# First batch's attention written as a function of its own, with k on two queues, w_in behind v, the second softmax in token halves, and weight conversions ordered behind h's copies

## The chip, the cores and the metric

The kernel runs on one core of a Trainium2 chip. The metric is the time of one execution in microseconds (us) on the device; the median of repeated runs is compared. Before the change the median of three runs is 793.76 us (792.74 to 795.01).

## The reference

Two computations follow each other. First, attention through 32 packed queries per head: with q, k, v of 8 batches, 8 heads, 576 tokens and 64 dimensions and p of 32 rows per head,

```python
def sm_attn(qq, kk, vv):
    s = scale * np.matmul(qq, kk.transpose(0, 1, 3, 2))
    s = s - np.max(s, axis=-1, keepdims=True)
    a = np.exp(s)
    a = a / (np.sum(a, axis=-1, keepdims=True) + 1e-09)
    return np.matmul(a, vv)
p_packed = sm_attn(p, k, v)
out = sm_attn(q, p_packed, p_packed)
```

Then a feed-forward layer on the 4608 tokens of 512 features, with w_in 512 x 2048 and w_out 2048 x 512, both handed over as float64:

```python
h = x @ w_in
sp = np.maximum(h, 0.0) + np.log1p(np.exp(-np.abs(h)))
g = h * erf(sp)
return (g @ w_out).astype(np.float32)
```

## The kernel before

**The algebra.** The second attention's output is a2 x pt, where pt is the packed result of one batch and a2 the second softmax. The kernel never makes x: it multiplies pt into w_in once per batch (w' = pt x w_in, four blocks of 512 columns, `w_prime`, L298) and then takes h = a2 x w' over 256 inner elements (`h_part`, L338). Matmul operands are split in a high and a low part (hi, lo; a2h, a2l; wph, wpl; gh, gl; woh, wol) and three products are summed.

**A unit of work** is one block of 128 of the 2048 inner features for one batch: 128 units. Each has 12 matmuls for h (two token halves of 288, six each), copies of h from PSUM by ScalarE (`hs`, L354), a gate (Softplus and Erf on ScalarE, the product and the split into gh and gl on VectorE, `gate_group`, L322), and 12 matmuls into four output accumulators (`o_part`, L368), some units later. Units are gated in groups; a group begins with two loads of ScalarE's function table. The last 64 of the 576 tokens of each unit go through memory (`rest`, written by SP in `split_g`, L313) and are multiplied for pairs of batches (`o_rest`, L387). The first two batches are worked in turns of 8 units (batch 0, 1, 0, 1), the others 16 units at a time.

**Attention of a batch** (`attention`, L149) is a generator of 14 stages: loads of p, k, v and q on SP's queue; scores `s` and their maximum, Exp and scaling (a1); transposes `t` and their copy to a1t; the product `p` with v and its copy to pt (L263); second scores `s` and their transposes to ta (L275); maximum and subtraction (L280, L281); Exp (L283); sum, reciprocal, product, transpose to tb, a2h (L293) and a2l (L294). Batch 0 runs it ahead of all else, with the first block of w_in loaded in two pairs of tiles (`load_w_in_pair`, L96): the first pair is sent between k and v, the second between v and q.

**Weights.** A float64 tile is loaded as 64-bit words and turned into float32 by `convert` (L88): one scaling on ScalarE (L91), which waits for the load, and three bit operations on VectorE (L92 to L94). A tile of w_out is also split (`split_w_out`, L116). The first four of these tiles go into free buffers of w' (`EARLY`), the others through two staging buffers (tag `wst`).

**What sets the order.** `PLAN` says after which unit each attention stage, w' block and weight load is written in the program, which units end a gate group (`ends`) and how many units later the outputs follow (`wait`). The Tile scheduler then orders each engine's queue by its own estimate of times; an engine executes its queue in that order. From unit 48 on (`strict`) TensorE's order is that of the program; ScalarE's table functions follow each other as written (`in_turn`).

Of the kernel before, what the change touches and what calls it, by code (L numbers as in the profile page):

```python
# [18 lines left out]
PLAN = {  # L19
    "att": {1: (1, 1, 2, 2, 3, 4, 4, 5, 5, 7, 7), 2: (15, 15, 19, 19, 20, 20, 22, 24, 25, 25, 25, 27, 28, 30)},  # L20
    "steady": (0, 0, 0, 1, 2, 2, 5, 6, 7, 9, 11, 11, 12, 13),
    "wp": (-1, 2, 6, 6, 14, 10, 22, 23),
    "wp_steady": (12, 14, 15, 20),
    "wi": {1: (0, 0, 2, 2), 2: (6, 9, 11, 11), 3: (11, 12, 14, 16)},
    "wo": (0, 1, 1, 2, 2, 3, 4, 6, 15, 15, 18, 20, 21, 22, 23, 26),
    "ends": (4, 5, 8, 12, 13, 16),
    "wait": (4, 1, 1, 1, 1),
    "strict": 48,
}
# [5 lines left out]
def tile_pack_attention_moe(ctx: ExitStack, tc: tile.TileContext, qT, kT, v, pT, w_in, w_out, out, rest):  # L35
# [51 lines left out]

    def convert(dst, low, high):  # L88

        bits = dst.bitcast(U32)  # L90
        nc.scalar.mul(dst, high.bitcast(F32), F64_SCALE)  # L91
        nc.vector.tensor_scalar(bits, bits, 3, None, op0=ALU.logical_shift_left)  # L92
# [1 line left out]
        nc.vector.scalar_tensor_tensor(bits, low, 29, bits, op0=ALU.logical_shift_right, op1=ALU.bitwise_or)  # L94
# [243 lines left out]
    def h_part(n, c):  # L338
# [8 lines left out]
        at_c = slice(c * HT, (c + 1) * HT)  # L347
        ps = ps_h.tile([P, 512], F32, name=f"h{b}_{f}_{c}", tag="ps_h")
        m = 0
        for r in range(2):  # L350
            for w, a in ((whi, ahi), (whi, alo), (wlo, ahi)):
                pe(nc.tensor.matmul(ps[:, 0:HT], w[:, r, fo:fo + P], a[:, r, at_c], start=(m == 0), stop=(m == 5)))  # L352
                m += 1
        nc.scalar.copy(hs[:, at_c], ps[:, 0:HT])  # L354
# [116 lines left out]
    gens[0], gens[1] = attention(0), attention(1)  # L471
    pairs = []
    next(gens[0])
    pairs.append(load_w_in_pair(0))
    next(gens[0])
    pairs.append(load_w_in_pair(2))
    next(gens[0])
    for _ in range(STAGES - 3):
        next(gens[0])
    for pair in pairs:  # L480
        if pair:
            convert(*pair)
    for _ in range(3):
        next(gens[1])
# [62 lines left out]
```

## Time and profile before

| | us |
|---|---|
| median of three runs (lowest, highest) | 793.76 (792.74, 795.01) |
| the profiled execution | 795.34 |
| its span, first to last instruction | 793.4 |
| TensorE busy in the span | 733.5 |
| ScalarE busy | 494.9 |
| VectorE busy | 435.5 |

The span is what the trace covers; the profiled execution's own time has 1.94 us more around it. PE is TensorE's matmul, PEld its weight load, DVE VectorE, ACT ScalarE, POOL GpSimd, SP the engine that issues most DMAs (SPq its queue). A timeline row reads: start, length, engine, line, operation, output <- inputs, shapes, count, and in brackets the idle time before it and what released it. The granted clock is TensorE's, as a share of full speed. In a row of a stretch each engine's busy time is followed by its count of instructions.

### The profile page before, as it was taken

The numbers are of one execution on the slowest core, as the hardware profiler recorded it, in microseconds if no ns is written. First come the engines' busy times: TensorE is split into PE (matmuls) and PEld (weight loads), VectorE is DVE, ScalarE is ACT, GpSimd is POOL, SyncE is SP. The second block draws the span as 40 slices with busy tenths as digits, with TensorE's granted clock in tenths as the row PEclk, the third lists the DMA queues.
The fourth block names the chain that finished last, engine by engine and source line by source line (L and its number), as shares of the span: only waits on it lengthen the run. The fifth ranks groups of instructions, "written<-read, shape, count | busy, mean of one in ns | idle before, by whom it ended". The sixth has DMA issues, their size and how long they took to land.

```text
span 793.4 us, 12893 instructions
## 1 busy us (share of the span) xinstructions
PE 733.5 (92%) x5008; PEld 577.0 (73%) x5008; DVE 435.5 (55%) x678; ACT 494.9 (62%) x802; POOL 8.0 (1%) x14
## 2 busy tenths in 40 slices
PE   3458978999999999999999999999999999999997
PEld 2237636777777877778877887778777788788885
DVE  3597987774575237653584236644484326744440
ACT  3169658787587636776676457676576556766731
POOL 0000000000100100000000000000000000000000
PEclk7568988999999999999999999999999999999999
DMA  9922463451532532025212332024212320003103
GB/s 310 313 104 83 150 189 92 121 189 45 151 58 64 113 99 69 16 60 170 67 41 66 117 96 69 16 59 147 90 41 64 117 66 12 16 14 98 41 21 119
DMA packets 66397, 74.77 MB, mean 94 GB/s; under 512 B 40224, under 2 KB 42272, under 8 KB 66336
## 3 DMA queue, kind: packets, MB, share of 16 engines
q1 hardware_dynamic: 65184, 71.86, 29.4%
q0 software_dynamic: 1152, 2.10, 1.8%
q8 instruction: 39, 0.64, 0.3%
q14 instruction: 22, 0.18, 0.1%
HBM read 54.00 MB, written 19.92 MB: 93 GB/s over the span
## 4 chain that ended last, share of the span: by engine, by line
PE 71%; ACT 11%; DMA 8%; DVE 6%; issue 2%; SPq 1%; DVEq 0%; ACTq 0%
PE o L374 37%; PE h L352 21%; PE or L398 5%; DMA v<-v 3%; DMA wi<-w_in 3%; PE wp L304 3%; ACT t L330 2%; PE p L258 2%; ACT L330 2%; ACT t L327 1%; ACT hs L354 1%; DMA g<-rest 1%; PE s L272 1%; ACT L327 1%; PE s L209 1%
## 5 line engine op out<-in xcount | busy, mean ns | idle before, releaser
L374 PE MATMUL o<-woh,gl 128*128 128x512 f32 x512 | 201.9, 394 | 1.1 <-DVE gl L317 1.0
L374 PE MATMUL o<-woh,gh 128*128 128x512 f32 x512 | 201.4, 403 | 1.6 <-ACT ob L379 1.1
L354 ACT COPY hs<-h 128x288 f32<-128x288 f32 x256 | 97.6, 398 | 168.5 <-PE h L352 167.3
L374 PE MATMUL o<-wol,gh 128*128 128x512 f32 x512 | 201.4, 393 | 0.0
L352 PE MATMUL h<-a2h,wph 128*128 128x288 f32 x512 | 155.4, 304 | 14.0 <-ACT hs L354 14.0
L332 DVE TENSOR_TENSOR hs<-t,hs 128x576 f32<-128x576 f32 x128 | 91.8, 754 | 114.1 <-ACT t L330 114.1
L352 PE MATMUL h<-a2l,wph 128*128 128x288 f32 x512 | 152.3, 298 | 1.6 <-DVE a2l L294 1.6
L352 PE MATMUL h<-a2h,wpl 128*128 128x288 f32 x512 | 152.0, 297 | 0.0
L352 PEld LDWEIGHTS h<-a2h,wph 128*128 128x128 f32 x512 | 96.8, 190 | 41.9 <-ACT hs L354 24.7
L374 PEld LDWEIGHTS o<-woh,gh 128*128 128x128 f32 x512 | 95.6, 188 | 43.1 <-issue 26.9
L374 PEld LDWEIGHTS o<-wol,gh 128*128 128x128 f32 x512 | 96.4, 188 | 25.0 <-issue 4.4
L316 DVE CAST gh<-hs 128x576 fp32r<-128x576 f32 x128 | 58.2, 456 | 100.1 <-PE o L374 95.4
L374 PEld LDWEIGHTS o<-woh,gl 128*128 128x128 f32 x512 | 96.5, 188 | 17.5 <-DVE gl L317 2.3
L352 PEld LDWEIGHTS h<-a2l,wph 128*128 128x128 f32 x512 | 97.1, 190 | 9.7 <-DVE a2l L294 2.0
L352 PEld LDWEIGHTS h<-a2h,wpl 128*128 128x128 f32 x512 | 97.3, 190 | 0.9 <-issue 0.9
L317 DVE TENSOR_TENSOR gl<-hs,gh 128x576 fp32r<-128x576 f32 x128 | 96.3, 754 | 2.3
L327 ACT ACTIVATE t<-hs 128x576 f32<-128x576 f32 x128 | 88.0, 687 | 2.8
L330 ACT ACTIVATE t<-t 128x576 f32<-128x576 f32 x128 | 78.1, 675 | 0.4
L304 PE MATMUL wp<-w_in_sb,pt 64*32 64x512 f32 x512 | 47.9, 642 | 4.8 <-DVE wpl L307 3.3
L307 DVE TENSOR_TENSOR wpl<-wp,wph 128x1024 fp32r<-128x1024 f32 x32 | 39.1, 1222 | 17.8 <-ACT wph L306 17.2
L327 ACT ACT_TABLE_LOAD x36 | 46.2, 1283 | 0.6
L330 ACT ACT_TABLE_LOAD x36 | 46.2, 1283 | 0.6
(84 smaller groups left out, 569.4 us busy)
## 6 DMA issues: line engine op xcount, KB each, us to landing
q<-qT SPq DMA_DIRECT2D x32, 288.0 KB, 4.3
v<-v SPq DMA_DIRECT2D x32, 256.0 KB, 4.1
wos<-w_out SPq DMA_DIRECT2D x16, 512.0 KB, 3.5
out<-ob SPq DMA_DIRECT2D x32, 256.0 KB, 2.2
g<-rest SPq DMA_DIRECT2D x16, 512.0 KB, 3.3
k<-kT SPq DMA_DIRECT2D x28, 288.0 KB, 3.9
wi<-w_in SPq DMA_DIRECT2D x12, 512.0 KB, 4.6
rest<-gh SPq DMA_DIRECT2D x128, 32.0 KB, 1.5
```

Of the source, the lines that this page charges most:

```text
L258: pe(nc.tensor.matmul(po[64 * r:64 * r + 64, NK * c:NK * c + NK], values[j][0:n, 64 * (2 * c + r):64 * (2 * c + r) + 64], a1t[0:n, j, r, N ...
L304: pe(nc.tensor.matmul(ps[NK * c:NK * c + NK, r, :], pt[b][64 * r:64 * r + 64, NK * c:NK * c + NK], w_in_sb[64 * r:64 * r + 64, c, j * FB:( ...
L307: nc.vector.tensor_tensor(lo[:], ps[:], hi[:], op=ALU.subtract)
L316: nc.vector.tensor_copy(ghi[:], hs[:])
L317: nc.vector.tensor_tensor(glo[:], hs[:], ghi[:], op=ALU.subtract)
L327: in_turn(nc.scalar.activation(t[:], hs[:], AF.Softplus))
L330: in_turn(nc.scalar.activation(t[:], t[:], AF.Erf))
L332: nc.vector.tensor_tensor(hs[:], t[:], hs[:], op=ALU.mult)
L352: pe(nc.tensor.matmul(ps[:, 0:HT], w[:, r, fo:fo + P], a[:, r, at_c], start=(m == 0), stop=(m == 5)))
L354: nc.scalar.copy(hs[:, at_c], ps[:, 0:HT])
L374: pe(nc.tensor.matmul(acc[b][x][:], gg[:, x * P:(x + 1) * P], w[:], start=(first and n == 0), stop=(last and n == 2)))
L398: pe(nc.tensor.matmul(acc["rest"], gg, w[:], start=(k == 0 and i == 0 and n == 0), stop=(k == NFB - 1 and i == PER - 1 and n == 2)))
```

## The change

Batch 0's attention becomes a function `first_attention` with its own statements in their own order; `attention` keeps the other batches. The second and fourth tile of k are sent by ScalarE's queue ahead of its table load. All of v is sent before both pairs of w_in. The first softmax keeps scores in PSUM as before, but sums and scales each half of the rows apart. The transposes are copied out by ScalarE and VectorE, one half each. The second softmax (maximum, subtraction, Exp, sum, product, transpose, a2h, a2l) runs once for each half of the tokens, and the first half of h needs the first half only; a2 has its halves outermost for that. The list `hold` takes the names of the last a1t copy, of the second a2h copy and of every copy of h; a conversion's start on ScalarE is ordered behind the last of them written so far, without a semaphore.

`PLAN` has new numbers. Batch 1's loads, scores and first softmax are written right behind batch 0's attention, its remaining stages after units 1 to 7 (before: scores from unit 1 on, end at unit 7). Units 0 and 1 are gated by themselves, and the first outputs follow after unit 6 instead of 7.

```diff
-    "wi": {1: (0, 0, 2, 2), 2: (6, 9, 11, 11), 3: (11, 12, 14, 16)},
-    "ends": (4, 5, 8, 12, 13, 16),
+    "wi": {1: (0, 0, 2, 3), 2: (7, 7, 10, 13), 3: (12, 14, 16, 16)},
+    "ends": (2, 5, 7, 9, 12, 14, 16),
+    "hold": 1,
...
     def convert(dst, low, high):
...
+        start = nc.scalar.mul(dst, high.bitcast(F32), F64_SCALE)
+        if hold:
+            follow(start, hold[-1])
...
+    def first_attention():
...
+        for c in range(NC):
+            sent = (nc.scalar if c % 2 else nc.sync).dma_start(k[c][:], kT[0, :, c, :])
+        follow(nc.scalar.preload_act_table_set("exp_and_others"), sent.ins.name)
...
+        for j in range(NCH):
+            n = min(P, S - j * P)
+            nc.sync.dma_start(values[j][0:n, 0:2 * NC * 64], v[0, j * P:j * P + n, :])
+        staged = [load_w_in_pair(0), load_w_in_pair(2)]
...
+            if j % 2:
+                made = at[:, j - 1:j + 1].rearrange("p j r k -> p (j r k)")
+                hold.append((nc.scalar.copy if j == 1 else nc.vector.tensor_copy)(made, turned[j // 2]).ins.name)
+        hold.pop()
...
+        hold.append(nc.scalar.copy(at[0:REM, NT].rearrange("p r k -> p (r k)"), pr[0:REM, 0:2 * P]).ins.name)
+        yield
+        convert(*staged[0])
+        convert(*staged[1])
...
+        for x in range(2):
+            blocks = ta[:, x, :].rearrange("p (n k) -> p n k", k=NK)
...
+            in_turn(nc.scalar.activation(ta[:, x, :], ta[:, x, :], AF.Exp, scale=SCALE))
...
+            nc.vector.transpose(tb[:, x, :], ta[:, x, :])
+            done = nc.scalar.copy(hi[:, x, :], tb[:, x, :])
+            if x == PLAN["hold"]:
+                hold.append(done.ins.name)
+            nc.vector.tensor_tensor(lo[:, x, :], tb[:, x, :], hi[:, x, :], op=ALU.subtract)
...
-        nc.scalar.copy(hs[:, at_c], ps[:, 0:HT])
+        hold.append(nc.scalar.copy(hs[:, c * HT:(c + 1) * HT], ps[:, 0:HT]).ins.name)
```

**ScalarE's queue from its start.** Before, conversions of w_in (L91) stand ahead of the first Exp (L229), between it and the copies to a1t, and ahead of the second Exp (L283):

```order
L73 ACT_TABLE_LOAD
L91 ACTIVATE w_in_sb<-w_in_sb 128x2x512
L229 ACTIVATE a_0_119,ms_142<-s_0_0_0_122,m_120 128x288
L229 ACTIVATE a_0_119,ms_142<-s_1_0_0_132,m_120 128x288
L229 ACTIVATE a_0_119,ms_142<-s_0_0_1_123,m_120 128x288
L229 ACTIVATE a_0_119,ms_142<-s_1_0_1_133,m_120 128x288
L91 ACTIVATE w_in_sb<-w_in_sb 128x2x512
L185 COPY a1t_157<-t_0_158 128x1024
L253 COPY a1t_157<-p_1_169 64x256
L91 ACTIVATE w_in_sb<-wi_2_429 128x512
L283 ACTIVATE ta_215<-ta_215 128x1152
```

Now (L194 the first Exp, L208 and L212 the copies to a1t, L97 the conversions, L249 the second Exp, L166 the loads of k):

```order
L166 DMA k_0_87<-kT 128x576
L166 DMA k_0_89<-kT 128x576
L167 ACT_TABLE_LOAD
L194 ACTIVATE a_0_119,ms_120<-s_0_123,m_121 128x288
L194 ACTIVATE a_0_119,ms_120<-s_1_0_124,m_121 128x288
L194 ACTIVATE a_0_119,ms_120<-s_0_123,m_121 128x288
L194 ACTIVATE a_0_119,ms_120<-s_1_1_125,m_121 128x288
L208 COPY a1t_158<-t_0_0_159 128x512
L212 COPY a1t_158<-p_161 64x256
L97 ACTIVATE w_in_sb<-w_in_sb 128x2x512 x2
L249 ACTIVATE ta_225<-ta_225 128x576 x2
```

The two conversions of the first block stand together behind the a1t copies, the third is no longer ahead of the second Exp, and two DMA issues stand in front.

**VectorE's queue around the copy of pt.** Before, the second pair's three steps (L92 to L94) stand ahead of pt's copy (L263):

```order
L231 SCALAR_TENSOR_TENSOR sm_121<-ms_142 128x2
L237 RECIPROCAL sm_121<-sm_121 128x2
L239 TENSOR_SCALAR a_0_119<-a_0_119,sm_121 128x576 x2
L92 TENSOR_SCALAR w_in_sb<-w_in_sb 128x2x512
L93 SCALAR_TENSOR_TENSOR w_in_sb<-w_in_sb 128x2x512
L94 SCALAR_TENSOR_TENSOR w_in_sb<-w_in_sb 128x2x512
L263 COPY pt_213<-p_0_168 128x128
L275 STREAM_TRANSPOSE ta_215<-s_0_0_0_216 128x288
```

Now (L100 to L102 the steps of the conversion, L225 pt's copy, L241 the first transpose of the second scores):

```order
L196 SCALAR_TENSOR_TENSOR sm_122<-ms_120 128x1
L197 RECIPROCAL sm_122<-sm_122 128x1
L198 TENSOR_SCALAR a_0_119<-a_0_119,sm_122 128x576
L208 COPY a1t_158<-t_0_1_160 128x512
L100 TENSOR_SCALAR w_in_sb<-w_in_sb 128x2x512
L101 SCALAR_TENSOR_TENSOR w_in_sb<-w_in_sb 128x2x512
L100 TENSOR_SCALAR w_in_sb<-w_in_sb 128x2x512
L102 SCALAR_TENSOR_TENSOR w_in_sb<-w_in_sb 128x2x512
L101 SCALAR_TENSOR_TENSOR w_in_sb<-w_in_sb 128x2x512
L102 SCALAR_TENSOR_TENSOR w_in_sb<-w_in_sb 128x2x512
L225 COPY pt_223<-p_161 128x128
L241 STREAM_TRANSPOSE ta_225<-s_0_0_230 128x288
```

Both pairs' six steps stand between the first softmax and pt's copy, where one pair's three stood. Further on, from batch 0's last a2l to batch 1's a2l, VectorE has 79 instructions where it had 88; TensorE has issued 64 output matmuls by batch 1's first h where it had issued 96.

**SP's queue, where loads of weights meet the first writes to `rest`.** Before (`wi` tiles of w_in, `wos` of w_out):

```order
L83 DMA wos_340<-w_out 128x512
L83 DMA wos_368<-w_out 128x512
L83 DMA wi_3_435<-w_in 128x512
L83 DMA wi_0_327<-w_in 128x512
L83 DMA wi_1_333<-w_in 128x512
L191 DMA p_2205<-pT 128x128
L83 DMA wos_442<-w_out 128x512
L83 DMA wos_453<-w_out 128x512
L83 DMA wos_542<-w_out 128x512
L83 DMA wos_591<-w_out 128x512
L320 DMA rest<-gh_0_514 128x64
```

Now:

```order
L87 DMA wos_384<-w_out 128x512
L87 DMA wos_432<-w_out 128x512
L87 DMA wi_0_371<-w_in 128x512
L87 DMA wi_1_377<-w_in 128x512
L307 DMA p_2247<-pT 128x128
L436 DMA rest<-gh_0_418 128x64
L436 DMA rest<-gl_0_419 128x64
L436 DMA rest<-gh_1_425 128x64
L436 DMA rest<-gl_1_426 128x64
L87 DMA wos_488<-w_out 128x512
L87 DMA wi_3_587<-w_in 128x512
L87 DMA wos_594<-w_out 128x512
```

The four writes of units 0 and 1 (gh and gl of each) stand ahead of the last tile of w_in's second block (wi_3) and of further tiles of w_out, which before stood ahead of all writes.

More of the change, by code (lines that the diff above doesn't have):

```diff
@@ L19 @@
 PLAN = {
[L20 to L23, printed above, removed]
-    "wi": {1: (0, 0, 2, 2), 2: (6, 9, 11, 11), 3: (11, 12, 14, 16)},
-    "wo": (0, 1, 1, 2, 2, 3, 4, 6, 15, 15, 18, 20, 21, 22, 23, 26),
-    "ends": (4, 5, 8, 12, 13, 16),
-    "wait": (4, 1, 1, 1, 1),
+    "att": {1: (-1, -1, -1, -1, -1, -1, -1, 1, 2, 2, 2, 2, 4, 7), 2: (14, 19, 19, 19, 19, 21, 22, 23, 26, 26, 28, 29, 30, 31)},
+    "steady": (1, 1, 1, 1, 2, 6, 6, 6, 7, 9, 11, 12, 13, 13),
+    "wp": (-1, 1, 4, 5, 14, 3, 22, 23),
+    "wp_steady": (12, 14, 14, 20),
+    "wi": {1: (0, 0, 2, 3), 2: (7, 7, 10, 13), 3: (12, 14, 16, 16)},
+    "wo": (0, 1, 2, 2, 3, 3, 4, 7, 16, 18, 19, 19, 23, 23, 24, 24),
+    "ends": (2, 5, 7, 9, 12, 14, 16),
+    "wait": (5, 3, 4, 4, 2),
     "strict": 48,
+    "first": 4,
+    "hold": 1,
 }
@@ L72, in tile_pack_attention_moe, with follow @@
     wo, wo_hi, wo_lo = {}, {}, {}
-    nc.scalar.preload_act_table_set("exp_and_others")
-    make_identity(nc, ident)
+    def follow(ins, name):
+        tc.add_manual_dep(ins.ins, name, mybir.DependencyInfo(
+            mybir.DependencyClass.NoSync, mybir.DependencyReason.DATA), reason="order")
     def load_f32(dst, src, name, pool=None, tag="wst"):
@@ L127, in in_turn @@
         if functions:
-            tc.add_manual_dep(ins.ins, functions[-1], mybir.DependencyInfo(
-                mybir.DependencyClass.NoSync, mybir.DependencyReason.DATA), reason="table")
+            follow(ins, functions[-1])
         functions.append(ins.ins.name)
+        return ins.ins.name
     pe_last, strict = [], [False]
@@ L136, in pe @@
         if strict[0] and pe_last:
-            tc.add_manual_dep(ins.ins, pe_last[-1], mybir.DependencyInfo(
-                mybir.DependencyClass.NoSync, mybir.DependencyReason.DATA), reason="order")
+            follow(ins, pe_last[-1])
         pe_last[:] = [ins.ins.name]
@@ L149, in attention @@
+    AT = {1: ("wo", "wo", "kvq")}
     def attention(b):
@@ L294, in attention @@
         nc.vector.tensor_tensor(lo[:], tb[:], hi[:], op=ALU.subtract)
-        a2[b] = (hi, lo)
+        a2[b] = tuple(y[:].rearrange("p r (x s) -> p r x s", x=2) for y in (hi, lo))
         yield
@@ L346, in h_part @@
         ahi, alo = a2[b]
-        at_c = slice(c * HT, (c + 1) * HT)
         ps = ps_h.tile([P, 512], F32, name=f"h{b}_{f}_{c}", tag="ps_h")
@@ L432, in tile_pack_attention_moe @@
     for b in range(1, B):
-        for n in PLAN["att"].get(b) or [first_use[b] - NF + n for n in PLAN["steady"]]:
-            at(n, ("att", b))
+        for i, n in enumerate(PLAN["att"].get(b) or [first_use[b] - NF + n for n in PLAN["steady"]]):
+            at(n, ("att", b, i))
     for k, (b, j) in enumerate(uses):
@@ L438, in tile_pack_attention_moe @@
             n = max(n, last_use[uses[k - NW]])
-        at(max([n] + [m for m, its in plan.items() if any(it[0] == "wi" and it[1] == j for it in its)]), ("wp", b, j))
+        at(max([n] + [m for m, its in plan.items() if any(it[0] == "wi" and it[1] == j for it in its)]), ("wp", b, j)) if k else None
     gens = {}
@@ L449, in do @@
                     gens[b] = attention(b)
-                if b == 1:
+                if b == 1 and it[2] >= PLAN["first"]:
                     with tc.high_priority():
@@ L464, in do @@
                     split_w_out(it[1])
-            elif it[1:] == (0, 0):
-                with tc.high_priority():
-                    w_prime(0, 0)
             else:
                 w_prime(it[1], it[2])
[L471 to L484, printed above, removed]
+    gens[0] = first_attention()
+    for _ in gens[0]:
+        pass
     do(plan.pop(-1))
```

87 lines of the change are left out of this document (84 added, 3 removed).

## The prediction

> **What bounds the kernel now.** I read the page first, then the busy time by stretches, then the waits, and last the timeline of each engine in the first 50 us. The page gives the profiled execution: a span of 793.4 us inside a run of 795.34 us, so 1.94 us lie around the span. That run is 1.58 us above the median of the three runs shown (793.76).
>
> ```profile
> span 793.4 us, 12893 instructions
> PE 733.5 (92%) x5008; PEld 577.0 (73%) x5008; DVE 435.5 (55%) x678; ACT 494.9 (62%) x802; POOL 8.0 (1%) x14
> ```
>
> TensorE is busy for 92% of the span, and the change leaves its work as it is. What can be won is idle time of TensorE. The busy time by stretches (columns: length, PE busy, PEld, DVE, ACT, POOL, granted clock, DMA share, GB/s) says where that lies.
>
> ```profile
> 0.00:48.80 48.80, 18.97 (x205) 10.12 (x205) 27.38 (x44) 15.11 (x25) 0.70 (x6) 0.61 0.83 282
> 48.80:110.40 61.60, 52.90 (x373) 37.06 (x373) 53.05 (x88) 44.01 (x71) 0.00 (x0) 0.88 0.38 120
> 110.40:200.00 89.60, 82.04 (x545) 63.44 (x544) 60.75 (x103) 70.39 (x118) 0.00 (x0) 0.93 0.40 121
> 200.00:300.00 100.00, 100.00 (x691) 78.25 (x690) 47.84 (x73) 61.45 (x101) 7.32 (x8) 0.95 0.39 93
> 300.00:793.40 493.40, 479.58 (x3202) 388.13 (x3200) 246.46 (x372) 303.93 (x487) 0.00 (x0) 0.95 0.23 68
> ```
>
> TensorE idles 48.80 - 18.97 = 29.8 us before 48.8, 8.7 us up to 110.4, 7.6 us up to 200, and nothing from 200 to 300. From the last units of batch 2 (near 260 us) on, TensorE's order is the same in both kernels, so what idles there (13.8 us after 300) stays. The whole change is a matter of the first 200 us, and what is won there arrives at the end undiminished, because TensorE is full from 200 to 300.
>
> In the second stretch VectorE, not TensorE, is fullest: 53.05 of 61.60 us, 86%. The waits between 48.8 and 140 us (total, times, longest) show what TensorE idles for:
>
> ```profile
> ACT w_in_sb L91 <- DMA wi<-w_in: 13.4, 6, 4.1
> PE h L352 <- ACT hs L354: 8.6, 7, 3.0
> PE wp L304 <- DVE wpl L307: 3.3, 2, 2.4
> ```
>
> ScalarE stands 13.4 us in front of weight conversions whose loads have not landed, and h's copies stand behind them.
>
> **The change part by part.** *The first attention.* First ScalarE, then TensorE, then VectorE in the first 49 us (start, length, what):
>
> ```profile
> 10.77 1.12 ACT L91 ACTIVATE w_in_sb<-w_in_sb 128x1024 f32<-128x1024 f32 x1 [8.75 <-DMA w_in_sb<-w_in]
> 11.79 0.49 ACT L229 ACTIVATE a<-s,m 128x288 f32<-128x288 f32 x1
> 13.21 0.52 ACT L229 ACTIVATE a<-s,m 128x288 f32<-128x288 f32 x1
> 17.10 1.14 ACT L91 ACTIVATE w_in_sb<-w_in_sb 128x1024 f32<-128x1024 f32 x1 [3.27 <-DMA w_in_sb<-w_in]
> 19.21 0.36 ACT L253 COPY a1t<-p 64x256 f32<-64x256 f32 x1
> 34.72 0.66 ACT L91 ACTIVATE w_in_sb<-wi 128x512 f32<-128x512 f32 x1 [15.15 <-DMA wi<-w_in]
> 35.28 1.15 ACT L283 ACTIVATE ta<-ta 128x1152 f32<-128x1152 f32 x1
> 45.01 1.15 ACT L293 CAST a2h<-tb 128x1152 fp32r<-128x1152 f32 x1
> ```
>
> ```profile
> 8.26 1.19 PE L209 MATMUL s<-k,p 64*32 64x288 f32 x8 [0.28 <-DMA k<-kT]
> 19.36 4.62 PE L258 MATMUL p<-a1t,v 128*64 128x32 f32 x80 [0.89 <-ACT a1t L185]
> 24.38 2.17 PE L272 MATMUL s<-q,pt 64*32 64x288 f32 x32 [0.39 <-DVE pt L263]
> 48.80 0.61 PE L352 MATMUL h<-a2l,wph 128*128 128x288 f32 x1 [1.65 <-DVE a2l L294]
> ```
>
> ```profile
> 10.75 0.17 DVE L224 TENSOR_SCALAR m<-m 128x2 f32<-128x2 f32 x1
> 11.92 0.69 DVE L92 TENSOR_SCALAR w_in_sb<-w_in_sb 128x1024 uint32<-128x1024 uint32 x1 [1.00 <-ACT w_in_sb L91]
> 13.91 1.23 DVE L94 SCALAR_TENSOR_TENSOR w_in_sb<-w_in_sb 128x1024 uint32<-128x1024 uint32 x1
> 15.05 0.15 DVE L231 SCALAR_TENSOR_TENSOR sm<-ms 128x2 f32<-128x2 f32 x1
> 15.44 0.95 DVE L239 TENSOR_SCALAR a<-a,sm 128x576 f32<-128x576 f32 x2
> 24.04 0.29 DVE L263 COPY pt<-p 128x128 f32<-128x128 f32 x1 [2.56 <-PE p L258]
> 25.71 1.80 DVE L275 STREAM_TRANSPOSE ta<-s 128x288 f32<-128x288 f32 x4 [1.38 <-PE s L272]
> 27.54 1.35 DVE L280 TENSOR_REDUCE mx<-ta 128x36 f32<-128x1152 f32 x1
> 28.93 1.36 DVE L281 TENSOR_TENSOR ta<-ta,mx 128x1152 f32<-128x1152 f32 x1
> 42.72 1.37 DVE L290 STREAM_TRANSPOSE tb<-ta 128x1152 f32<-128x1152 f32 x1
> 47.39 1.35 DVE L294 TENSOR_TENSOR a2l<-tb,a2h 128x1152 fp32r<-128x1152 f32 x1
> ```
>
> ```profile
> 1.19 1.84 SPq L165 DMA_DIRECT2D k<-kT  x4
> ```
>
> ```profile
> L307 DVE TENSOR_TENSOR wpl<-wp,wph 128x1024 fp32r<-128x1024 f32 x32 | 39.1, 1222 | 17.8 <-ACT wph L306 17.2
> ```
>
> The first row is SP's issue of k, the second the page's group for the remainder of w'. The chain is walked with these lengths.
>
> **k.** SP issues four loads in 1.84 us. Two of them move to ScalarE, so the last is issued about 0.9 us earlier; the DMA engines are nearly full then (share 0.83 over the stretch, start included), so the last k may land no earlier. I take -0.5 (bounds 0 and -0.9): 7.8 instead of 8.26. The Trainium skill (DMA: Bandwidth & Descriptors, "Issuing engines are not separate DMA queues") says that loads started from several engines share the same 16 DMA engines, so only issue time is saved; by that this term is at most the 0.9, and the sum below would be 0.4 us lower. Before has no second queue, so its trace cannot say.
>
> **First softmax.** From the last k to m ready it takes 10.92 - 8.26 = 2.7 us: 10.5. Before, Exp then waits for a conversion on ScalarE until 11.79, and the row sums wait for a conversion on VectorE until 15.05. Both conversions leave this place. Four Exp take 13.21 + 0.52 - 11.79 = 1.9 us, the last half's sum and scaling about 0.9 (0.15 + 0.17 + half of 0.95 and gaps): 13.4 instead of 16.4.
>
> **Transposes and copies** took 19.57 - 16.39 = 3.2 us; one copy moves to VectorE, so 2.7: the product with v starts at 16.1 and ends at 20.8 (4.62 us).
>
> **pt does not follow at once.** On VectorE both pairs' conversions now stand ahead of pt's copy, and their starts on ScalarE are held behind the last copy of a1t, at 16.2. First start 1.1 us, then two times 15.14 - 11.92 = 3.2 us on VectorE: pt's copy starts at 23.8 and ends at 24.1, against 24.33. Nearly all of the 4 us won so far is lost here. The second pair's load landed at 17.10 before; the same bytes lie ahead of it, so it is no later than its turn.
>
> **Second softmax in halves.** Before, from 24.33 to 48.74 it takes 24.4 us. Exp's operand is ready at 30.29 and Exp starts at 35.28, because the conversion ahead of it waits for its load until 34.72: 5.0 us that go. Conversions stand among its VectorE steps: they go too. What is left is 1.4 us to s and then VectorE's own steps: four transposes 1.8, maximum 1.4, subtraction 1.4, sum 1.4, product 1.4, transpose 1.4, remainder 1.4 (halves cost half each), w' remainder 1.2 and about 1.7 of small steps and waits for the two copies to a2h (0.6 each, half of 1.15): 14.5 in all. The end is at 38.6.
>
> So a2's second half is ready at 38.6 instead of 48.74: -10.1 us (bounds -8 with k at 8.26 and two waits between halves, -13 if VectorE overlaps more).
>
> *From there to batch 1.* This lead is not the gain: h can start, but weights are needed too. Before had converted three weight tiles and part of two more by 48.8; now the conversions are held behind h's copies. I count VectorE's work from a2l of batch 0 to a2l of batch 1, the point at which batch 1's h may start. Before, a2l of batch 1 ends here:
>
> ```profile
> 109.27 1.36 DVE L294 TENSOR_TENSOR a2l<-tb,a2h 128x1152 fp32r<-128x1152 f32 x1
> ```
>
> It is 88 instructions in 53.05 us of busy time, at 86% of the stretch. In the changed order 79 stand there (fewer gates and conversions), so 53.05 x 79/88 = 47.6 us, at the same 86% 55.4 us: a2l of batch 1 at 94.0. I take 95, since two new waits fall on VectorE here: the gate of units 0 and 1 stands ahead of the third to sixth weight conversions, and SP sends four rest writes of that gate ahead of the next weight loads, w_in's fourth tile among them. At 95% full it would be 88.7, at 75% 102. Lead here: 110.6 - 95 = 15.6.
>
> *What is left to do there.* By that point TensorE had issued 96 output matmuls before, 64 in the changed order. Their price in the chain of the late part:
>
> ```profile
> 744.69 0.79 PE h L352 x6
> 745.47 1.37 PE o L374 x6
> ```
>
> 32 x 1.37/6 = 7.3 us, with a part of a w' product about 8 us of work that is still to be done: +8.
>
> *Up to 200 us.* Before idles 7.6 us there. The eight us of deferred work can fill such holes, but 14 more conversion steps also remain on VectorE, which is busy for 60.75 of 89.6 us and has room. I take half: -3 (bounds -7.6 and +3).
>
> **Sum:** -15.6 + 8 - 3 = -10.6 us. 795.34 - 10.6 = 784.7 for a run like the profiled one; against the median, which is 1.6 lower, 793.76 - 10.6 = 783.2.
>
> The clock is a second price of idling: it was granted at 0.61 in the first stretch and 0.88 in the second. The Trainium skill (TensorE: Matmul & The Clock Gate, "Part 1: The HAM clock gate") has TensorE fall to half rate after an idle window of about 3.4 us and return after as long a busy one; the rows' direction agrees. What it would do is the second rival.
>
> **The rivals.**
>
> *First, the holes close.* The deferred output matmuls cover all idle time up to 200 us, and VectorE runs at 95%: -21.9 + 8 - 7.6 = -21.5 at the far end; I count from -14 to -20, about 777. For it: every ScalarE wait of the 13.4 us for loads is in front of h's copies. Against: gates, table loads and conversions still share two in-order engines.
>
> *Second, half clock.* The fifth unit's weights are some 50 VectorE steps behind 38.6: 50 x 0.60/0.86 = 35 us, 73.6. Until then TensorE has only h of four units (48 x 0.79/6 = 6.3 us), two units of output (24 x 1.37/6 = 5.5) and batch 1's attention (about 5): 17 us of work in 35. If the holes keep it at half rate, this takes 34 us, and every further us that TensorE waits on the way makes the fifth unit late; with 4 or 5 us of such waits the gain is -6, 787.8. For it: 0.61 in the stretch with such holes. Against: the second stretch of before had holes too, at 0.88.
>
> *Third, the lead is given back.* VectorE is the limit, and the conversions put off must all be paid before 130 us: 14 steps of 0.6 us, 8.4 of the 10.6. Then nothing that can be measured is left. The first attention is not by itself after all: pt's copy still waits for weight conversions, and later ones can stand in front of h's copies as before.
>
> *Fourth, weights too late: slower.* Later weight loads wait for a staging buffer and for the rest writes ahead of them on SP. Before, such loads went out at this pace:
>
> ```profile
> 87.78 0.33 SPq L83 DMA_DIRECT2D wi<-w_in  x1
> 98.53 0.33 SPq L83 DMA_DIRECT2D wi<-w_in  x1
> ```
>
> 10.75 us from one to the next. Batch 1's a2l has five staged loads ahead of it, two buffers at a time, the first when the gate of units 0 and 1 is through, 27 steps behind 38.6, near 58. If every pair takes 14 us or more and the order behind it is not caught up, a2l comes at 58 + 3 x 14 + 14 (20 steps of 0.6 us at 86%) = 114, 3.4 us later than before, and with +8 and -7.6 the run is 3.8 us slower: 797.6. It decides from 106 us on for a2l. Against it: these loads here wait for conversions that are held behind copies made early.
>
> **How the numbers follow.** The forecast (-6 to -14) gets 0.55, rival 1 0.15, rival 2 0.15, rival 3 0.07, rival 4 0.08. Everything but the last two is faster. 0.3%, what a measurement of this kernel can tell from no change, is 2.4 us; so faster 0.85, same 0.07, slower 0.08. The range holds the forecast, rival 2 and the near half of rival 1: from -17.8 (776) to -2.8 (791).
>
> **What would show it.** In the changed profile: Exp of the first softmax near 10.5 and no conversion before it; pt's copy near 24 with the two pairs' conversions just ahead of it; a2l's second half near 38.6; the granted clock of 40 to 70 us; batch 1's a2l near 95; TensorE without idle time from 200 to 300, and the stretch from there to the end as long as before (within 1 us). It is wrong if batch 1's a2l comes after 105 or before 88, if idle time up to 200 us behind it is not below 7.6, or if the late part changes its length.

## The result, and the profile after

The changed kernel takes 784.99 us (median of 4 runs, 784.06 to 787.61) against 794.24 us before (4 runs, 792.74 to 795.01): a ratio of 0.989 with a 95% interval of 0.9867 to 0.9914, so 9.25 us or 1.1% less. The profiled execution took 785.28 us (span 783.4 us), against 795.34 us (span 793.4 us): 10.06 us less. Steps are compared within these two profiles.

The page of the changed kernel gives its engines, and the busy time by the same stretches as before (columns as before: PE, PEld, DVE, ACT, POOL, clock, DMA share, GB/s) says where the time came from.

```profile
PE 732.7 (94%) x5008; PEld 581.9 (74%) x5008; DVE 436.6 (56%) x689; ACT 496.8 (63%) x806; POOL 8.0 (1%) x14
```

```profile
0.00:48.80 48.80, 26.01 (x238) 17.33 (x238) 28.92 (x54) 20.27 (x37) 0.69 (x6) 0.96 0.76 271
48.80:110.40 61.60, 51.82 (x370) 38.32 (x369) 53.67 (x89) 45.34 (x70) 0.00 (x0) 0.87 0.36 113
110.40:200.00 89.60, 85.85 (x575) 68.49 (x575) 63.56 (x109) 73.52 (x125) 0.00 (x0) 0.98 0.46 138
200.00:300.00 100.00, 100.00 (x710) 77.44 (x709) 52.86 (x80) 64.59 (x102) 7.31 (x8) 1.00 0.40 100
300.00:783.40 483.40, 469.03 (x3121) 380.32 (x3119) 237.56 (x360) 293.10 (x474) 0.00 (x0) 1.00 0.22 67
```

TensorE's busy time is 0.8 us less than before (733.5), its idle time 9.2 us less (793.4 - 733.5 = 59.9, now 783.4 - 732.7 = 50.7). By stretches it now idles 22.8, 9.8, 3.8, 0 and 14.4 us, before 29.8, 8.7, 7.6, 0 and 13.8. The second stretch is no better: VectorE has 89 instructions and 53.67 us there, before 88 and 53.05. It is the order of that work that differs: batch 1's attention comes first.

The first attention on TensorE, VectorE and ScalarE (start, length, what):

```profile
5.29 3.05 PE L186 MATMUL s<-k,p 64*32 64x288 f32 x32 [5.29 <-DMA k<-kT]
15.68 4.63 PE L220 MATMUL p<-a1t,v 128*64 128x32 f32 x80 [0.46 <-ACT a1t L212]
```

```profile
12.90 0.52 DVE L198 TENSOR_SCALAR a<-a,sm 128x576 f32<-128x576 f32 x1
16.70 0.69 DVE L100 TENSOR_SCALAR w_in_sb<-w_in_sb 128x1024 uint32<-128x1024 uint32 x1 [0.95 <-ACT w_in_sb L97]
21.56 1.23 DVE L102 SCALAR_TENSOR_TENSOR w_in_sb<-w_in_sb 128x1024 uint32<-128x1024 uint32 x1
22.70 0.28 DVE L225 COPY pt<-p 128x128 f32<-128x128 f32 x1
36.56 0.76 DVE L258 TENSOR_TENSOR a2l<-tb,a2h 128x576 fp32r<-128x576 f32 x1 [0.74 <-ACT a2h L255]
59.22 0.28 DVE L379 COPY pt<-p 128x128 f32<-128x128 f32 x1
93.38 1.35 DVE L410 TENSOR_TENSOR a2l<-tb,a2h 128x1152 fp32r<-128x1152 f32 x1
```

```profile
10.44 0.50 ACT L194 ACTIVATE a<-s,m 128x288 f32<-128x288 f32 x1 [7.49 <-DVE m L191]
```

No conversion stands before Exp. The two pairs' conversions run from 16.70 to 22.8 us, just ahead of pt's copy, although the product with v ended at 20.3. Batch 0's a2 ends at 37.3 us (before 48.7), batch 1's at 94.7 (before 110.6).

What sets that 94.7 is in the chain of waits, followed back from there (start, length, what; left out at the marks are small pieces and VectorE's steps, of which more below):

```profile
60.16 3.77 DMA wi<-w_in
63.95 0.75 ACT w_in_sb L97
...
67.24 0.57 DVE w_in_sb L102
...
72.00 1.15 DVE wpl L423
73.19 2.30 PE h L467 x8
...
76.44 0.58 ACT t L443
77.03 1.28 ACT L446
78.33 0.69 ACT t L446
```

A weight load is in it: the fourth tile of w_in's second column block. SP issues it at 60.16 us, because its staging buffer comes free then (the conversion before it ends at 59.42 + 0.68 us on VectorE). Its conversion makes w' of that block, w' the fifth unit's h, that unit closes a gate, and batch 1's second Exp stands behind this gate on ScalarE, since the functions are kept in the order in which they were written.

The load is only one part of this chain. From 64.72 to 73.15 us and from 79.05 us to a2's end it runs along VectorE's queue, 24.1 of the 34.6 us from the load's issue to a2:

```profile
82.04 1.16 ACT L399 ACTIVATE ta<-ta 128x1152 f32<-128x1152 f32 x1
84.07 1.35 DVE L401 TENSOR_REDUCE mx<-ta 128x36 f32<-128x1152 f32 x1
```

Exp ends at 83.20, and the sum over its result (L401) starts 0.87 us later, behind gate and conversion steps that stand ahead of it on VectorE. From 79.05 to 94.73 us VectorE is busy for 15.65 of 15.68 us: there its own queue is the limit.

### The profile page after: what moved, and what is told of

The parts are those of the page before. It is cut to its first block, busy times and chain, and to the rows that moved or that the text cites. A ratio compares the mean times of both kernels' runs of the same rounds, so it can differ in the third digit from the quotient of the medians.

```text
span 783.4 us, 12901 instructions
## 1 busy us (share of the span) xinstructions
PE 732.7 (94%) x5008; PEld 581.9 (74%) x5008; DVE 436.6 (56%) x689; ACT 496.8 (63%) x806; POOL 8.0 (1%) x14
## 4 chain that ended last, share of the span: by engine, by line
PE 73%; ACT 12%; DVE 10%; DMA 3%; issue 2%; SPq 0%; DVEq 0%; ACTq 0%
PE o L489 38%; PE h L467 22%; PE or L513 5%; PE wp L420 3%; ACT t L446 2%; PE p L374 2%; ACT L446 2%; DVE hs L448 2%; ACT t L443 2%; ACT hs L469 1%; DMA g<-rest 1%; ACT L443 1%; PE s L325 1%; DVE ta L397 1%; DVE mx L396 1%
## 5 line engine op out<-in xcount | busy, mean ns | idle before, releaser
L467 PE MATMUL h<-a2h,wph 128*128 128x288 f32 x512 | 158.6, 310 | 18.0 <-ACT hs L469 10.4
L467 PE MATMUL h<-a2h,wpl 128*128 128x288 f32 x512 | 154.2, 302 | 1.0 <-DVE wpl L423 1.0
L467 PE MATMUL h<-a2l,wph 128*128 128x288 f32 x512 | 154.6, 302 | 0.0
L467 PEld LDWEIGHTS h<-a2h,wph 128*128 128x128 f32 x512 | 99.7, 195 | 47.0 <-ACT hs L469 16.2
L489 PEld LDWEIGHTS o<-woh,gh 128*128 128x128 f32 x512 | 96.6, 189 | 41.2 <-issue 23.8
L489 PEld LDWEIGHTS o<-wol,gh 128*128 128x128 f32 x512 | 96.3, 188 | 23.0 <-issue 2.1
L467 PEld LDWEIGHTS h<-a2l,wph 128*128 128x128 f32 x512 | 99.9, 195 | 10.0 <-DVE mx L252 0.9
L467 PEld LDWEIGHTS h<-a2h,wpl 128*128 128x128 f32 x512 | 99.8, 195 | 2.4 <-DVE wpl L423 1.3
L446 ACT ACTIVATE t<-t 128x576 f32<-128x576 f32 x128 | 78.1, 674 | 0.4
L420 PE MATMUL wp<-w_in_sb,pt 64*32 64x512 f32 x512 | 44.3, 646 | 6.3 <-ACT a L301 3.4
```

The costliest lines, as they stand in the source:

```text
L420: pe(nc.tensor.matmul(ps[NK * c:NK * c + NK, r, :], pt[b][64 * r:64 * r + 64, NK * c:NK * c + NK], w_in_sb[64 * r:64 * r + 64, c, j * FB:( ...
L446: in_turn(nc.scalar.activation(t[:], t[:], AF.Erf))
L489: pe(nc.tensor.matmul(acc[b][x][:], gg[:, x * P:(x + 1) * P], w[:], start=(first and n == 0), stop=(last and n == 2)))
```

## Theories, and the experiments

The prediction's theory: the gain is made by the first attention's own chain and by how much VectorE work lies between batch 0's a2 and batch 1's. Rivals: the new table of numbers makes it; the order that holds conversions behind copies does not matter; TensorE's half pace (its matmuls for h start 0.24 us apart instead of 0.13) decides. The last four runs test a theory formed after the first eight: from 50 us on the chain through the weight load above decides. The runs came in three groups of four, each beside the kernel before on the same chip (median 792.28, 793.44 and 793.25 us). All ratios are to the kernel before.

**e1: the new function with the old table.** All of the table's entries change but `strict` and `hold`; two are shown.

```diff
-    "att": {1: (-1, -1, -1, -1, -1, -1, -1, 1, 2, 2, 2, 2, 4, 7), 2: (14, 19, ...
+    "att": {1: (-1, -1, -1, 1, 1, 2, 2, 3, 4, 4, 5, 5, 7, 7), 2: (15, 15, ...
...
-    "ends": (2, 5, 7, 9, 12, 14, 16),
+    "ends": (4, 5, 8, 12, 13, 16),
```

> The changed kernel with the old table of numbers (batch 1's attention starts with three stages, the rest at the old places). Theory (the gain is made by the first attention's own chain, the table only lays the rest behind it): a2's second half again within 0.5 us of the 37.3 us of the changed kernel, and at least half of the 9.25 us stays, 785 to 790 us. Rival (the table makes the gain, by moving batch 1's attention forward): 791 to 796 us, although a2 is early.

801.13 us, ratio 1.0112 (1.0088 to 1.0135): slower than before, which neither theory had. In its profile pt of batch 1 is copied at 82.5 us (59.22 in the changed kernel), and its a2 is late:

```profile
110.05 1.36 DVE L410 TENSOR_TENSOR a2l<-tb,a2h 128x1152 fp32r<-128x1152 f32 x1 [1.22 <-ACT a2h L409]
```

Batch 0's a2 is as early as in the changed kernel (37.9 us); by batch 1's a2 (111.4) the whole lead is gone.

**e2: the old function with the new table.** The table as in the changed kernel, the rest as before (first softmax, loads and conversions included).

```diff
-    "att": {1: (1, 1, 2, 2, 3, 4, 4, 5, 5, 7, 7), 2: (15, 15, 19, ...
+    "att": {1: (-1, -1, -1, -1, 1, 2, 2, 2, 2, 4, 7), 2: (14, 19, 19, ...
...
-    "ends": (4, 5, 8, 12, 13, 16),
+    "ends": (2, 5, 7, 9, 12, 14, 16),
```

> The kernel before with the new table of numbers; attention of batch 0 by the old function, two loads of k on one queue, no order between conversions and copies. Theory (first attention): a2 of batch 0 ends no earlier than 44 us, and the time is 792 to 800 us. Rival (table): 784 to 789 us.

802.26 us, 1.0122 (1.0103 to 1.0142). The rival is out: the table alone costs 10 us. That its a2 would end no earlier than 44 us was narrowly wrong (43.7), and the time lies above the theory's 792 to 800. So the two parts can't be priced one by one: +8.9 us and +10.0 us alone, -9.3 us together.

**e3: k on one queue.**

```diff
-            sent = (nc.scalar if c % 2 else nc.sync).dma_start(k[c][:], kT[0, :, c, :])
+            sent = nc.sync.dma_start(k[c][:], kT[0, :, c, :])
```

> The changed kernel with all four loads of k issued by SP; the order on ScalarE, VectorE and TensorE stays as it is. Theory (the second queue is worth its issue time, about 0.9 us, and all that follows shifts by it): the first products with k end 0.4 to 0.9 us later, a2's second half at 37.7 to 38.2 us, 785.3 to 786.2 us. Rival A (the loads share the same DMA engines, nothing is won): the products end within 0.2 us, 785.0 us. Rival B (loads on one queue hold v and w_in back as well): over 787 us.

787.27 us, 0.9922 (0.9902 to 0.9943), an interval that overlaps the changed kernel's. The products with k, on one queue:

```profile
4.17 4.53 PE L186 MATMUL s<-k,p 64*32 64x288 f32 x32 [4.17 <-DMA k<-kT]
```

They start 1.1 us earlier than with two queues and end at 8.70 instead of 8.34; what follows is no later (Exp at 10.31 against 10.44, a2 at 36.9 against 37.3). Nothing in this profile speaks for the second queue's 0.5 us; the median leaves room for it and for more. The median lies in rival B's range, but what B gives as the reason does not show: the product with v starts at 15.25 us (15.68 with two queues), and the first conversion of w_in on ScalarE at 15.10 (15.53).

**e4: no order between conversions and copies; e4b: that order only up to a2's copy.**

```diff
-        if hold:
-            follow(start, hold[-1])
```

```diff
-        hold.append(nc.scalar.copy(hs[:, c * HT:(c + 1) * HT], ps[:, 0:HT]).ins.name)
+        nc.scalar.copy(hs[:, c * HT:(c + 1) * HT], ps[:, 0:HT])
```

> The changed kernel without the rule that a conversion's start on ScalarE is held behind the last copy of a1t, a2's copy or h's copies. The order then has a conversion between the first softmax and its copy, one between the two halves' Exp, and three ahead of a2's second half and h's first copy. Theory (conversions whose loads have not landed stop the chain on ScalarE): a2's second half at 40 to 46 us and 788 to 792 us. Rival (the rule matters little, the loads land in time): a2's second half before 39 us, 784 to 786.5 us.

> The changed kernel with the rule for conversions kept up to a2's copy, but not behind h's copies: a2 stays early, and three conversions then stand ahead of h's first copy. Theory (most of the rule's worth is behind a2, where it keeps ScalarE free for h's copies and batch 1's first softmax): a2's second half at 37.3, batch 1's a2 at 100 us or later, 790 to 800 us. Rival (the rule's worth is in a2 alone): 784 to 787 us.

e4 takes 803.28 us, 1.0139 (1.0121 to 1.0156), e4b 801.31 us, 1.01 (1.0085 to 1.0114): the rule is worth more than the whole gain, and most of it behind a2. Both times lie above the ranges of the theory (788 to 792 and 790 to 800). In e4b, a2 of batch 0 is untouched, and batch 1's first attention is late:

```profile
69.44 0.28 DVE L379 COPY pt<-p 128x128 f32<-128x128 f32 x1
110.18 1.35 DVE L410 TENSOR_TENSOR a2l<-tb,a2h 128x1152 fp32r<-128x1152 f32 x1
```

pt comes 10.2 us later than in the changed kernel, a2 of batch 1 16.8 us later. In e4 (line numbers two lower) a2 of batch 0 ends at 44.2 us, as the theory had it, batch 1's at 110.3. e2 lacks the rule as well, and e4, which has the new function, is no faster than e2 (803.28 and 802.26 us): without the rule the new function gains nothing over the old one. The old function with the new table and the rule was not run.

**e5: pt's copy ahead of the second pair's conversion.** The first pair stays in its place; the second pair's first VectorE step follows the copy.

```diff
-        convert(*staged[1])
...
+        copied = nc.vector.tensor_copy(ptt[:], po[:, 0:P])
...
+        convert(*staged[1], after=copied.ins.name)
```

> The changed kernel with pt's copy on VectorE ahead of the second pair's conversion instead of behind it; ScalarE's order and the table stay. Theory (pt waits 2.4 us for conversions, and what is won there arrives): pt copied near 20.6 us instead of 23.0, a2's second half 1.0 to 2.4 us earlier than 37.3, and 783 to 784.3 us. Rival (from there VectorE's and ScalarE's other work sets the time, as the jointly chosen table leaves it): a2 earlier by as much, but batch 1's a2 still at 94 to 96 us and 784.5 to 787 us.

788.47 us, 0.9932 (0.9912 to 0.9952). The chain moved as expected, and it bought nothing, as the rival said, though both numbers lie above the rival's ranges:

```profile
20.21 0.29 DVE L226 COPY pt<-p 128x128 f32<-128x128 f32 x1 [0.46 <-PE p L221]
97.13 1.35 DVE L412 TENSOR_TENSOR a2l<-tb,a2h 128x1152 fp32r<-128x1152 f32 x1
```

pt 2.5 us earlier, a2 of batch 0 1.9 us earlier (35.4), a2 of batch 1 at 98.5 instead of 94.7 (98.8 in the control below). The order behind a2 changed as well: between the two a2 VectorE has 85 instructions and 50.18 us of work, 80 and 47.18 us in the changed kernel. So the run does not price the earlier pt by itself.

**e6: batch 0's second softmax in whole steps**, from the maximum to a2's remainder.

```diff
-        for x in range(2):
-            blocks = ta[:, x, :].rearrange("p (n k) -> p n k", k=NK)
+        for _ in range(1):
+            blocks = ta[:].rearrange("p x (n k) -> p (x n) k", k=NK)
```

> The changed kernel with batch 0's second softmax in whole steps instead of halves. Theory (halves let VectorE work on one while ScalarE has the other): a2 ends at 39.5 to 41.5 us instead of 37.3, and the time is 786 to 789 us. Rival (VectorE is full there either way, and whole steps cost less in all than two halves): a2 at 37 to 38.5 us and 784 to 786 us.

801.1 us, 1.0094 (1.0077 to 1.0111). a2 of batch 0 is late as expected (40.8 us, of which pt's start, 24.91 instead of 22.70, makes 2.2 and the whole steps 1.3), but the time is 12 us beyond the theory's bound. In its profile VectorE, SP and TensorE show why:

```profile
67.41 0.85 DVE L390 STREAM_TRANSPOSE ta<-s 128x288 f32<-128x288 f32 x2 [4.04 <-PE s L387]
69.93 0.69 DVE L102 SCALAR_TENSOR_TENSOR wo<-wos,wo 128x512 uint32<-128x512 uint32 x1
```

```profile
70.68 0.33 SPq L87 DMA_DIRECT2D wi<-w_in  x1
```

```profile
79.11 1.92 PE L419 MATMUL wp<-w_in_sb,pt 64*32 64x512 f32 x4 [6.50 <-DVE w_in_sb L102]
```

The load of w_in's fourth tile goes out 10.5 us later than in the changed kernel (60.16); w' of that block waits 6.5 us for it. A load of batch 2's k stands ahead of it on SP (70.00), but the chain of waits puts the load's start down to the last step of a w_out tile's conversion, which ends at 70.62. That step stands on VectorE behind the first transposes of batch 1's second scores, for which VectorE waited 4.04 us. This is what led to the new theory.

**e8: TensorE's hole behind the second unit filled.** 16 matmuls more, into unused columns of an h tile, in order behind the second unit's last h and ahead of the third's first.

```diff
+        for _ in range(16):
+            ins = nc.tensor.matmul(ps[:, HT:512], w[:, 0, 0:P], a[:, 0, 0, 0:512 - HT], start=True, stop=True,
+                                   skip_group_check=True)
+            follow(ins, after)
+            after = ins.ins.name
```

> The changed kernel with 16 more matmuls (unused columns of an h tile) where TensorE stands idle for 3.6 us behind the second unit's h; they take part in nothing. Rival 2 of the prediction (TensorE's half pace after such a hole costs time): the next h matmuls start 0.13 us apart instead of 0.24, and the time is 1 to 3 us less, 782 to 784 us. Theory (VectorE and ScalarE set the pace up to batch 1's a2): whatever h's pace there, batch 1's a2 stays at 94 to 96 us and the time at 784.5 to 786.5 us.

785.64 us, 0.9901 (0.9883 to 0.9918), batch 1's a2 at 96.3: the time that the theory gave, a2 0.3 us past its range. The hole is shortened from 3.63 to 2.48 us, not closed. It does not refute the rival, since the pace changed for only seven of the matmuls behind the hole; from 46.84 us on they start 0.24 us apart again:

```profile
45.78 0.40 PE L478 MATMUL h<-a2h,wph 128*128 128x288 f32 x1 [2.48 <-ACT hs L485]
...
46.84 0.44 PE L478 MATMUL h<-a2l,wph 128*128 128x288 f32 x1
```

**e13: the changed kernel once more, beside e10 to e12.** Nothing is changed.

> The changed kernel once more, beside the three others on the same chip. Every theory: a ratio to the kernel before within 0.3% of the 0.989 measured first, 783 to 787.5 us; what it differs by from run to run is what differences of 1 to 3 us between experiments are worth.

786.53 us, 0.991 (0.988 to 0.9941), single runs from 783.07 to 790.85 us; the profiled one took 790.28 us, with batch 1's a2 at 98.8 where the first profile of the same kernel had 94.7. Differences of 1 to 3 us between experiments are not to be read as effects.

**e12: the load of w_in's fourth tile one place later.** One w_out tile goes ahead of it on SP.

```diff
-    "wo": (0, 1, 2, 2, 3, 3, 4, 7, 16, 18, 19, 19, 23, 23, 24, 24),
+    "wo": (0, 1, 2, 2, 2, 3, 4, 7, 16, 18, 19, 19, 23, 23, 24, 24),
```

> The changed kernel with the same load one place later on SP, behind one more w_out tile, so that it waits for one more free buffer (from 60.2 to about 64.3 us). New theory (the chain through this load): its conversion at 67 to 70 us instead of 64, batch 1's second Exp at 85 to 92 us instead of 82.0, its a2 at 98 us or later, 787 to 800 us. Rival A (VectorE's work as a whole): batch 1's a2 at 94 to 96 us and 784.5 to 786.5 us.

794.58 us (12 runs), 1.0011 (0.9998 to 1.0025): one of the table's hundred numbers takes the whole gain. In e12's profile the chain of waits is:

```profile
66.24 4.42 DMA wi<-w_in
70.68 0.67 ACT w_in_sb L97
...
75.05 1.94 PE wp L420 x4
...
78.08 2.60 PE h L467 x8
...
87.68 1.16 ACT ta L399
```

```profile
108.20 1.35 DVE L410 TENSOR_TENSOR a2l<-tb,a2h 128x1152 fp32r<-128x1152 f32 x1
```

Against e13 (load issued at 61.91, the fifth unit's h at 72.3, Exp at 83.4, a2 of batch 1 at 98.8; batch 0's a2 within 0.2 us in both) the load is 4.3 us later, h 5.8, Exp 4.2, a2 10.8 and the median 8.1 us. So the later load fits Exp's 4.2 us. The other 6.5 of a2's 10.8 arise between Exp and a2, and there VectorE's order has changed too. The stretches from Exp's end to a2's end, in the changed kernel, e13, e12 and e10 (columns as above):

```profile
83.20:94.73 11.53, 10.51 (x66) 8.10 (x66) 11.50 (x17) 10.62 (x18) 0.00 (x0) 1.00 0.23 61
84.60:98.79 14.19, 13.19 (x66) 10.30 (x66) 11.62 (x17) 10.52 (x18) 0.00 (x0) 0.76 0.17 50
88.84:109.55 20.71, 20.38 (x99) 15.47 (x98) 17.55 (x25) 13.78 (x21) 0.00 (x0) 0.86 0.19 54
82.13:102.39 20.26, 19.06 (x99) 15.58 (x98) 18.22 (x28) 14.86 (x22) 0.00 (x0) 0.92 0.19 54
```

In e12 VectorE has 25 instructions and 17.55 us of work there, in e13 17 and 11.62 us: the conversions of two later w_in tiles now stand ahead of a2's remainder. The one number moved more than a load.

**e10: the same load earlier**, in the place of a w_out tile.

```diff
-    "wi": {1: (0, 0, 2, 3), 2: (7, 7, 10, 13), 3: (12, 14, 16, 16)},
+    "wi": {1: (0, 0, 2, 2), 2: (7, 7, 10, 13), 3: (12, 14, 16, 16)},
```

> The changed kernel with one number of the table changed: the fourth tile of w_in's second column block is loaded earlier, in the place of one w_out tile, which goes where it stood (25.7 and 60.2 us on SP). New theory (from 50 us on the chain is: this load, its conversion, w' of that block, the fifth unit's h, its gate, batch 1's second Exp, which stands behind that gate, and batch 1's a2): its conversion at 51 to 54 us instead of 64, that Exp at 78 to 81 us instead of 82.0, and 782 to 784.5 us. Rival A (VectorE's work as a whole sets batch 1's a2): Exp within 1 us of 82, 784.5 to 786.5 us. Rival B (the table holds only as a whole, any other order loses): over 790 us.

789.2 us, 0.995 (0.993 to 0.997): no gain, so here the new theory is wrong on the time, although the conversion and Exp (81.0) came when it said. ScalarE's step of the tile is done by 52.1 us (it began at 63.95 in the changed kernel), yet w' of that block starts where it did:

```profile
67.53 1.09 PE L420 MATMUL wp<-w_in_sb,pt 64*32 64x512 f32 x16 [1.67 <-DVE ta L391]
```

It now waits for ta alone: w' and batch 1's scores share one PSUM slot. In the changed kernel w' waited for ta too (to 67.39 us), and the last step of the tile's conversion ended at 67.8; both ways in are equally late there, so making one earlier wins nothing and making it later costs at once. Why a2 of batch 1 ends 20.3 us after Exp here, and 11.5 in the changed kernel, is in the stretches above: VectorE has 28 instructions, where the changed kernel has 17, and is busy for 18.22 us of 20.26. Steps of two w_in tiles and of w_out tiles are among them. So 6.7 of the 8.7 us are work that now stands ahead of a2, the rest a wait of 2.02 us for the next gate. Why the scheduler put it there stays open.

**e11: the old places for batch 1's attention alone.**

```diff
-    "att": {1: (-1, -1, -1, -1, -1, -1, -1, 1, 2, 2, 2, 2, 4, 7), 2: (14, 19, ...
+    "att": {1: (-1, -1, -1, 1, 1, 2, 2, 3, 4, 4, 5, 5, 7, 7), 2: (14, 19, ...
```

> The changed kernel with the old places for batch 1's attention alone; all other numbers of the table stay new. New theory (the lead is spent by batch 1's attention, which must start early; the table's part of the gain lies in that): batch 1's pt copied at 70 us or later instead of 59.2, its a2 at 105 us or later, 793 to 803 us. Rival (the chain through w_in's fourth tile alone decides, and that stays): batch 1's a2 at 95 to 98 us and 784 to 788 us.

806.04 us, 1.0149 (1.0132 to 1.0167), the slowest of all. The theory's direction holds beyond its range:

```profile
87.76 0.28 DVE L379 COPY pt<-p 128x128 f32<-128x128 f32 x1
118.91 1.36 DVE L410 TENSOR_TENSOR a2l<-tb,a2h 128x1152 fp32r<-128x1152 f32 x1 [1.22 <-ACT a2h L409]
```

The fifth unit's h starts at 74.8 us, but Exp only at 110.0: here batch 1's attention itself is late.

All runs side by side, by the rows of their profiles (us; the fifth unit's h and Exp start, a2 ends; all columns but the median are of the one profiled execution):

| kernel | a2, batch 0 | fifth unit's h | second Exp, batch 1 | a2, batch 1 | VectorE busy between the two a2 | profiled execution | median |
|---|---|---|---|---|---|---|---|
| changed | 37.3 | 70.9 | 82.0 | 94.7 | 47.2 of 57.4 | 785.28 | 785.0 |
| e3 one queue | 36.9 | 70.5 | 81.7 | 95.9 | 47.3 of 59.0 | 787.41 | 787.3 |
| e8 hole filled | 37.3 | 71.2 | 82.4 | 96.3 | 47.6 of 59.0 | 784.79 | 785.6 |
| e5 pt first | 35.4 | 69.8 | 80.9 | 98.5 | 50.2 of 63.1 | 784.59 | 788.5 |
| e13 control | 39.1 | 72.3 | 83.4 | 98.8 | 47.2 of 59.7 | 790.28 | 786.5 |
| e10 load early | 37.8 | 70.1 | 81.0 | 102.4 | 51.9 of 64.6 | 788.38 | 789.2 |
| e12 load late | 39.3 | 78.1 | 87.7 | 109.6 | 53.7 of 70.3 | 794.66 | 794.6 |
| e2 table alone | 43.7 | 79.5 | 90.9 | 109.8 | 52.4 of 66.1 | 801.00 | 802.3 |
| e4 no order | 44.2 | 84.1 | 94.3 | 110.3 | 49.3 of 66.1 | 803.35 | 803.3 |
| e1 function alone | 37.9 | 68.3 | 100.2 | 111.4 | 56.6 of 73.6 | 799.99 | 801.1 |
| e4b order to a2 | 38.6 | 81.7 | 92.5 | 111.5 | 59.8 of 72.9 | 800.82 | 801.3 |
| e6 whole steps | 40.8 | 82.1 | 91.7 | 113.2 | 52.6 of 72.4 | 801.62 | 801.1 |
| e11 old places | 39.2 | 74.8 | 110.0 | 120.3 | 56.8 of 81.0 | 807.06 | 806.0 |

Batch 0's a2, the visible success of the change, does not sort the times (e1 and e4b have it early). Batch 1's a2 parts them in two groups, up to 102.4 us with 784 to 791 us and from 109.6 us on with 794 us and more; within the first group it sorts nothing (e5's execution took 784.59 us with 98.5, the control's 790.28 us with 98.8). The stretch between the two a2 is VectorE's work and its waits, and both differ: 47 to 48 us of work in the four profiles with the changed kernel's order (changed, e3, e8, e13), 49 to 60 in the others, and 10 to 24 us of waits. The spread from 794.6 to 803.3 us at the same 109 to 111 us, and the kernel before's 794.2 at 110.6, need a second cause. It may be how far units and output have got by then; that was not tested.

## Why the prediction was right, and where its reasons were not

The forecast (783.2 us, -10.6) holds: -10.06 us in the profiles, -9.25 in the medians.

- **k, -0.5:** not shown. e3 has no cost of one queue in its profile, and the control's k products ended 1.8 us later than those of the same code in the first profile. The term is below what one profile can tell.
- **First softmax and pt.** Exp predicted at 10.5, at 10.44; scaled by 13.4, at 12.90 + 0.52. pt's copy predicted at 23.8, measured 22.70 in one profile and 24.46 in the other: behind the conversions, as said. That this wait of 2.4 us could be removed for nothing was not claimed; e5, which removed it, shows no gain, with a changed order behind it.
- **a2 of batch 0:** predicted 38.6, measured 37.3 and, in the control, 39.1. The halves are worth 1.3 us of that chain (e6, from pt to the end).
- **a2 of batch 1:** predicted 95, measured 94.7 in this profile and 98.8 in the control's, so the 0.3 us are luck: the start was 1.3 us earlier than predicted, VectorE's share 82% instead of 86%, and 1 us had been added, which cancel. The count of VectorE's work was right: 47.6 us predicted, 47.18 us (80 instructions) measured between the two a2, 47.2 in the control. The reason given, that this work sets the time, is half the truth. For it: in the last 15.7 us before a2 VectorE does not pause, and in e10 more work ahead of a2 makes a2 late with Exp early. Against it: the share is no constant. It is 70 to 82% in the thirteen profiles of the table, and in e4 49.3 us of work go with 803 us. Of the 10.6 us by which e12's stretch between the two a2 is longer than the control's, 6.5 are work (53.72 us against 47.24) and 4.1 waits. What sets the waits is the chain through the weight load and batch 1's early attention, both laid out by the table. In its sum the prediction gave new waits 1 us, the rest writes ahead of w_in's fourth tile among them, and left the rest to its fourth rival.
- **Work left behind, +8, and idle up to 200 us, -3.** The three stretches behind a2 idle 0.3, 0 and 3.8 us, 4.1 where there were 7.6: -3.5.

```profile
95.00:110.40 15.40, 15.08 (x84) 12.17 (x83) 12.69 (x23) 12.50 (x20) 0.00 (x0) 1.00 0.37 115
110.40:140.00 29.60, 29.60 (x161) 23.34 (x161) 19.24 (x33) 24.07 (x39) 0.00 (x0) 1.00 0.42 124
140.00:200.00 60.00, 56.25 (x416) 45.14 (x415) 44.32 (x77) 49.45 (x87) 0.00 (x0) 0.97 0.47 145
```

  The work left behind would then be 15.9 - 10.06 + 3.5 = 9.3 us, predicted 8. It is what is left over in the sum; it was not measured by itself.
- **The late part** has its length: from batch 7's a2h (669.20 us) to the end it takes 114.2 us, before 113.9 (from 679.52).
- **Rival 2, half clock,** was half there: TensorE ran at half pace in parts of 36 to 52 and 67 to 79 us (granted clock 0.53 from 46 to 52, 0.50 from 67 to 79, 0.81 over the prediction's 40 to 70 us), and the fifth unit's weights came at 73.2 us (it had 73.6). The gain did not shrink to its -6. What the half pace costs is not shown, since e8 hardly changed it. One place can be read: w' of the fifth unit's block takes 2.40 us in the changed kernel, a wait for the last step of w_in's tile included, and 1.09 us in e10, and the h behind it starts 0.8 us earlier there.
- **Rival 4, weights too late behind rest writes and staging buffers,** got 0.08 and 797.6 us. It did not happen, but it is the mechanism that lies closest: e12 makes part of it happen with one number (794.6), and in e6 the same load waits for its staging buffer (801.1). The prediction held against it only that these loads wait for conversions behind copies made early, and did not see that the changed order has no slack there.
- **Third rival, the lead given back:** e1 and e4b do this in full.

## What to carry to other kernels

A table of places and the code that it places are one change: either half alone lost 9 to 10 us here (the rule for conversions counted with the code), so a change that brings both is judged by its final order on each engine, never by the sum of its parts. A lead at one milestone (batch 0's a2, 10 us) counts only if the next shared milestone moves: follow the chain back from that one, and look for the load whose buffer comes free last. Where two ways into a step are equally late, making one earlier wins nothing and delaying either costs at once; a utilisation read from the old profile (86%) cannot be carried over as a constant (70 to 82% in the runs here), since it holds the waits of the old order. An edit of one number in a table can reorder a queue that it does not name: compare the work ahead of the milestone before an effect is put down to the number.
